# Loading the first batch of a fused attention and feed-forward kernel unit by unit, with GpSimd kept to issuing loads in the opening

## The chip, the cores and the metric

The kernel runs on one core of one Trainium2 chip. The metric is the device time of one execution in microseconds (us); lower is better. The span of a profiled execution is shorter than its time (337.9 against 339.8 us for the kernel before), and both are used here, never one against the other.

## The reference

Causal attention in a sliding window of 64 over 8 batches, 8 heads, 576 positions and 64 channels, then a feed-forward layer with a rectified gate over the 4608 rows:

```
scores = (q @ k^T) / sqrt(64)          # q, k, v: [8, 8, 576, 64] fp32, inputs scaled by 0.1
mask   = (0 <= i - j < 64)
attn   = softmax(where(mask, scores, -1e9)) @ v
x      = attn.transpose(0, 2, 1, 3).reshape(4608, 512)
out    = (relu(x @ w_gate) * (x @ w_val)) @ w_out      # 512 x 1536, 512 x 1536, 1536 x 512
```

## The kernel before

Attention works in 24 **units** of 192 positions (three windows, all 8 heads), three to a batch. Two units make a **tile** of 384 rows of the feed-forward layer. A unit goes through scores (`st`), exp (`p`), the product with v (`pv`, with the sums of the softmax by matmuls with ones), the copy from PSUM (`xv`), and normalisation on VectorE (`sT`, `rT`, `rs`, then `xt`). `xt` is what the gate matmuls (`h<-xt,wg`) read. The **hidden part** of a tile is its gate and value matmuls (`wg`, `wv`), its **output** the matmuls with w_out (`op`). In the first units the mask comes into the scores by **bias** matmuls. **Warm-ups** (`heat`) are matmuls on zeros that keep TensorE busy. To **land** is to have arrived in full. Matmuls of both layers are woven together by a table of times, `W.at(t, ...)`, which sets the program order on each engine.

The opening loads all of batch 0's k and q, four heads to a load, transposes them on VectorE, and does units 0 and 1 side by side:

```python
def k_first(hh):                          # k of batch 0 in fp32 over the sync queue
    k32 = nat["k32", hh] = x_sb.tile([128, S // 32 * D], FP32, name="k32", bufs=2)
    nc.sync.dma_start(k32, k[0, G * hh:G * hh + G].rearrange("h (i j) d -> (h i) (j d)", i=32))
...
def v_load(u):                            # by GpSimd's queue
    b, uu = divmod(u, UB)
    for w in range(UB):
        k0 = U * uu + 64 * w
        nc.gpsimd.dma_start(v16s[uu][64:128, w, :, 0:64], v[b, :, k0:k0 + 64].rearrange("h p d -> p h d"))
... # the schedule of the opening
W.at(8.7, lambda: u_st(0, (0,)))
W.at(11.0, lambda: u_st(0, (1,)))
W.at(11.4, lambda: u_pv(0, (0, 1)))
W.at(11.5, lambda: u_pv(0, (2, 3)))
W.at(11.7, lambda: u_st(1))               # unit 1's scores, ahead of unit 0's normalisation
W.at(12.2, lambda: u_back(0))
W.at(12.5, lambda: u_norm(0))
W.at(12.6, lambda: u_pv(1))
...
W.at(21.0, lambda: v_ones(2, nc.vector))  # memsets of the next v buffers, on VectorE
W.at(21.0, lambda: v_ones(0, nc.vector))
```

The softmax here doesn't subtract the row's maximum and nothing guards it: scores larger than these inputs give would overflow.

## Time and profile before

| what | value |
|---|---|
| time, median (range) | 339.79 us (339.25 to 339.82) |
| profiled span, mean granted clock | 337.9 us, 1.00 but for 3.4 us at 0.50 in the opening |
| k of batch 0 lands | 4.37 and 5.76 us |
| q of batch 0 lands | 7.47 and 9.39 us |
| v of units 0 and 1 lands | 10.02 to 13.00 us |
| first gate matmul | 17.00 us |
| unit 1's first gate matmul | 21.12 us |
| third tile's output starts | 93.92 us, then a steady 25.95 us for most tiles |

"Lands" is the issue's start plus its time to landing in the trace. The prediction shows the page's shares, the chain and the windows. Timeline columns: start us, duration us, engine, source line, operation, written tile <- read tiles, shapes, count, and in brackets the idle time before and its releaser.

```profile
13.13 0.55 PE L249 MATMUL st<-qT,kT 32*128 32x64 f16 x48
...
17.00 2.72 PE L419 MATMUL h<-xt,wg 128*128 128x192 f16 x16 [0.53 <-DVE xt L356]
...
21.12 1.07 PE L419 MATMUL h<-xt,wg 128*128 128x192 f16 x11
```

The first line is unit 1's scores. They are done at 13.7 us, 3.3 us ahead of unit 0's first gate matmul, so that unit 1 follows with no wait on the third line (its x11 are those inside the view's window, of 16). The middle line shows the half clock: 2.72 us for 16 matmuls. Because of it TensorE comes to unit 1 late: unit 1's `xt` is done at 20.46, and its first gate matmul starts at 21.12.

### The profile page before, as it was taken

The page shows a single profiled execution, that of the slowest core. Times are in us where ns is not written, and L with a number is a line of the kernel's source. Part 1 is how long each engine was busy: PE and PEld are TensorE (multiplying, and loading weights), DVE is VectorE, ACT ScalarE, POOL GpSimd, SP SyncE. Part 2 cuts the span into 40 slices and gives each one's busy share as a digit, 9 for nine tenths or more (in the row PEclk, how much of TensorE's full clock was granted, in tenths as well). Part 3 has the DMA queues.
Part 4 walks back from the last instruction along what each step waited for, and adds up shares of the span by engine and source line. Part 5 has one row for each costly group of instructions (what it writes and reads, how often), then busy time and mean ns, then how long its engine had stood idle before and what let it go on. Part 6 is the DMA issues. An engine that isn't in the chain of part 4 may idle for free.

```text
span 337.9 us, 8605 instructions
## 1 busy us (share of the span) xinstructions
PE 325.5 (96%) x3522; PEld 197.3 (58%) x3522; DVE 260.3 (77%) x493; ACT 176.7 (52%) x383; POOL 74.0 (22%) x121
## 2 busy tenths in 40 slices
PE   8699998999999999999999999999999999999995
PEld 4485485856546656655655655654655664664653
DVE  5878878998998874897989974888889874884430
ACT  4546165745636646645555564564564664653321
POOL 8724341250213221320210410150120200000000
PEclk9989999999999999999999999999999999999999
DMA  8999998496343933491242853296214402001002
GB/s 214 178 206 193 204 203 135 31 139 98 24 77 49 158 51 71 29 185 70 17 53 73 111 75 98 18 143 123 17 10 111 32 3 93 2 2 71 24 0 94
DMA packets 52886, 29.44 MB, mean 87 GB/s; under 512 B 39280, under 2 KB 44272, under 8 KB 52848
## 3 DMA queue, kind: packets, MB, share of 16 engines
q0 software_dynamic: 47088, 18.29, 47.4%
q1 hardware_dynamic: 5616, 10.55, 8.7%
q8 instruction: 27, 0.44, 0.6%
q14 instruction: 11, 0.09, 0.1%
q10 hardware_dynamic: 144, 0.07, 0.1%
HBM read 37.75 MB, written 9.44 MB: 140 GB/s over the span
## 4 chain that ended last, share of the span: by engine, by line
PE 81%; DVE 13%; issue 3%; DMA 2%; ACT 0%; DVEq 0%; ACTq 0%; POOLq 0%
PE h L419 52%; PE op L433 21%; PE pv L311 5%; PE st L249 3%; DVE sT L341 2%; DVE qT L186 2%; DMA q<-in_q_dram 2%; DVE g_sb L407 2%; DVE kT L186 1%; DVE xt L356 1%; DVE rs L350 1%; DVE p L270 1%; PE op L465 1%; DVE v L118 1%; DVE rT L348 0%
## 5 line engine op out<-in xcount | busy, mean ns | idle before, releaser
L419 PE MATMUL h<-xt,wg 128*128 128x384 f16 (+1 forms) x640 | 117.5, 313 | 1.7 <-DVE xt L356 1.7
L419 PE MATMUL h<-xt,wv 128*128 128x384 f16 (+1 forms) x640 | 116.7, 311 | 1.0 <-DVE g_sb L407 1.0
L407 DVE TENSOR_TENSOR g_sb<-r_sb,h 128x384 f16<-128x384 f32 x144 | 78.3, 550 | 48.8 <-PE h L419 47.1
L404 ACT ACTIVATE r_sb<-h 128x384 f32<-128x384 f32 x144 | 70.2, 492 | 67.0 <-PE h L419 55.3
L433 PE MATMUL op<-wo,g_sb 128*128 128x512 f16 x420 | 93.0, 379 | 0.0
L192 POOL DMA_DIRECT2D v<-in_v_dram x72 | 49.5, 696 | 181.0 <-PE pv L311 95.3
L419 PEld LDWEIGHTS <-wg 128*128 128x128 f16 x640 | 61.5, 99 | 36.5 <-DVE xt L356 1.6
L419 PEld LDWEIGHTS <-wv 128*128 128x128 f16 x640 | 59.0, 98 | 31.7 <-issue 1.3
L433 PEld LDWEIGHTS <-g_sb 128*128 128x128 f16 x420 | 40.3, 98 | 46.6
L341 DVE STREAM_TRANSPOSE sT<-pv 64x384 f32<-64x384 f32 x88 | 51.1, 580 | 9.7 <-PE pv L311 7.7
L329 ACT COPY xv<-pv 64x384 f32<-64x384 f32 x88 | 41.6, 473 | 21.5 <-DVE sT L341 8.1
L440 ACT COPY o_sb<-op 128x512 f32<-128x512 f32 x35 | 20.5, 586 | 54.6 <-PE op L433 54.6
L263 ACT ACTIVATE p<-st 128x384 f16<-128x384 f32 x92 | 39.7, 492 | 4.2 <-PE st L249 4.1
L270 DVE TENSOR_TENSOR p<-p,mask 128x384 f16<-128x384 f16 x88 | 27.5, 352 | 0.3 <-ACT p L263 0.2
L350 DVE STREAM_TRANSPOSE rs<-rT 128x768 f32<-128x768 f32 x24 | 23.5, 978 | 0.8
L356 DVE TENSOR_TENSOR xt<-xv,rs 128x768 f16<-128x768 f32 x24 | 22.8, 948 | 0.8
L311 PEld LDWEIGHTS <-v 128*128 128x128 f16 x528 | 18.6, 98 | 4.2 <-issue 0.8
L186 DVE STREAM_TRANSPOSE kT<-k 128x576 f32<-128x576 f32 (+1 forms) x18 | 19.7, 1121 | 1.4 <-ACT k L179 1.3
L311 PE MATMUL pv<-p,v 128*128 128x64 f16 x528 | 19.7, 193 | 1.1 <-DVE p L270 0.6
L186 DVE STREAM_TRANSPOSE qT<-q 128x576 f32<-128x576 f32 x16 | 18.9, 1239 | 1.1 <-DMA q<-in_q_dram 1.1
L249 PEld LDWEIGHTS <-kT 32*128 32x128 f16 x1152 | 11.0, 92 | 10.0 <-issue 9.9
L249 PE MATMUL st<-qT,kT 32*128 32x64 f16 x1152 | 13.9, 189 | 2.3 <-DVE qT L186 2.0
(47 smaller groups left out, 91.8 us busy)
## 6 DMA issues: line engine op xcount, KB each, us to landing
out_dram<-o_sb SPq DMA_DIRECT2D x35, 256.0 KB, 2.0
q<-in_q_dram POOLq DMA_DIRECT2D x16, 288.0 KB, 8.1
v<-in_v_dram POOLq DMA_DIRECT2D x72, 64.0 KB, 3.2
k<-in_k_dram POOLq DMA_DIRECT2D x14, 288.0 KB, 6.1
wg<-in_moe_w_gate_dram POOLq DMA_DIRECT2D x3, 512.0 KB, 10.1
wv<-in_moe_w_val_dram POOLq DMA_DIRECT2D x3, 512.0 KB, 11.9
wo<-in_moe_w_out_dram POOLq DMA_DIRECT2D x3, 512.0 KB, 13.7
k<-in_k_dram SPq DMA_DIRECT2D x2, 576.0 KB, 4.0
```

The source lines that it names most:

```text
L186: nc.vector.transpose(dst.rearrange("p (i j) -> p j i", i=32)[:, j0:j1], src[:, j0:j1])
L192: nc.gpsimd.dma_start(v16s[uu][64:128, w, :, 0:64], v[b, :, k0:k0 + 64].rearrange("h p d -> p h d"))
L249: nc.tensor.matmul(d["st"][hh][g][:, c:c + 64], kT[rows, hh, ks + 64 * w:ks + 64 * w + 128, dh], qT[rows, hh, ks + 64 * w:ks + 64 * w + 64 ...
L263: nc.scalar.activation(d["p"][g].rearrange("p h c -> p (h c)"), d["st"][0][g][:, 0:2 * U], ACT.Exp, scale=scale)
L270: nc.vector.tensor_tensor(p, p, mask[:, None, :].to_broadcast([128, 2 * UB, 64]), MUL)
L311: nc.tensor.matmul(d["pv"][c % 2][:, c // 2, e, 64 * w:64 * w + 64], v16[:, w, 128 * h - 64 * e:128 * h - 64 * e + 128], d["p"][h % G][:, ...
L329: nc.scalar.copy(d["xs"][rows, n::2], d["pv"][n][rows, :, e, 0:U])
L341: nc.vector.transpose(to[64 * e:64 * e + 64, half::2], d["pv"][half][64 - 64 * e:128 - 64 * e, :, e, 0:U])
L404: nc.scalar.activation(part(r_sb), part(h1), ACT.Relu)
L407: nc.vector.tensor_tensor(g_sb[:, f:f + w, c0:c1], part(r_sb), part(h2), MUL)
L419: nc.tensor.matmul(h[:, b * n:b * n + n], wt[:, c, (f + b) * 128:(f + b) * 128 + 128], xt[:, c, c0:c1], start=(c == 0), stop=(c == NC - 1))
L433: nc.tensor.matmul(op, g_sb[:, f, bass.ds(sub * 128, 128)], wo[:, f], start=(f == 0), stop=(f == NF - 1))
```

## The change

The intent: unit 0 needs only its own 192 rows of k and q, so load those alone and first (sync queue), flip them on TensorE in place of VectorE, let GpSimd issue nothing but loads until the first tile's weights are under way, and move memsets and copies of v from VectorE to GpSimd. The core of the diff, with cuts marked:

```diff
-    def k_first(hh):
-        k32 = nat["k32", hh] = x_sb.tile([128, S // 32 * D], FP32, name="k32", bufs=2)
-        nc.sync.dma_start(k32, k[0, G * hh:G * hh + G].rearrange("h (i j) d -> (h i) (j d)", i=32))
+    JA = U * H // 128                       # 12: a partition takes 12 positions of one head
+    def all_rows(name, u):
+        src = (q if name == "q" else k)[0, :, U * u:U * u + U]
+        return src.rearrange("h (i j) d -> i h (j d)", j=JA)
+    def unit_flip(name, u):                 # 24 matmuls of 64 columns against a permuted identity
...
+                nc.tensor.matmul(to[64 * hh:64 * hh + 64, 64 * j:64 * j + 64],
+                                 nat[name, u][:, D * j:D * j + D],
+                                 turn[:, G * hh:G * hh + G], ...)
...  (the opening, in program order)
+        for name in "kq":
+            all_load32(name, 0, nc.sync)
+            all_tile(name, 0)
...
+        heat(6, units[0]["st"][3])          # warm-up matmuls
+        for name in "kq":
+            all_load(name, 1)
+        v_load(0, ((1, 0, 128), (3, 0, 64)))
+        v_load(1, ((3, 64, 128), (5, 0, 128)))
+        for wt, t in ((G3[0], 12.3), (V3[0], 14.9), (G3[1], 17.5)):
+            w_load(*wt, t)
...
+        v_fixed(1, nc.gpsimd)               # the memsets, now on GpSimd
+        unit_loads(3)
...
+        v_spread(0)
+        u_st(0)
+        for c in order:
+            u_exp(0, c)
+        heat(6, flipped["k", 0][:, 1])
+        u_pv(0)
...
+        u_back(0)
+        u_norm(0)
+        v_spread(1)
+        heat(3, flipped["k", 0][:, 1])
+        for name in "kq":
+            unit_flip(name, 1)
+            for cc in range(2):
+                unit_keep(name, 1, cc, act)
+        heat(4, flipped["k", 1][:, 1, 256:512])
+        u_bias(1)
+        u_st(1)
+        v_spread(2, pool)
...
-        W.at(21.0, lambda: v_ones(2, nc.vector))
-        W.at(21.0, lambda: v_ones(0, nc.vector))
...
-            output_by_rows(0); ready(3); hidden(1, 0, U)      # abridged
+            ready(3); hidden(1, 0, U); output_by_rows(0)      # abridged
```

## The prediction

> **What bounds the kernel now.** I read the page's busy shares first, then its chain, then three views of the opening: the table of windows, the waits, and the timeline. The page says that TensorE is the bound of the whole:
>
> ```profile
> PE 325.5 (96%) x3522; PEld 197.3 (58%) x3522; DVE 260.3 (77%) x493; ACT 176.7 (52%) x383; POOL 74.0 (22%) x121
> PE 81%; DVE 13%; issue 3%; DMA 2%; ACT 0%; DVEq 0%; ACTq 0%; POOLq 0%
> ```
>
> The second line is the chain that ended last: 81% TensorE, and the 13% VectorE are where a gain could hide. The chain in order of time shows that the steady part is closed: from the third tile on, the 36 output matmuls of successive tiles start at 94.09, 120.04, 146, 172.65, 198.60 us, a period of 25.95 or 26.65 us. Work of one tile: 96 gate and value matmuls of 384 columns at 0.1625 us are 15.6, 36 output matmuls at 0.216 are 7.77, two units of attention at 0.48 + 0.70 are 2.4; 25.8 us. So nine tenths of the span cannot move, and the change must earn its keep before the third tile, at about 75 us. There, three things are lost. The windows of the opening (length, then busy time and count of PE, PEld, DVE, ACT, POOL, then the granted clock, DMA share, GB/s):
>
> ```profile
> 16.64:20.05 3.41, 3.04 (x20) 2.80 (x20) 3.24 (x8) 1.75 (x6) 0.76 (x1) 0.51 1.24 206
> 36.30:54.00 17.70, 17.70 (x208) 12.73 (x206) 14.38 (x25) 7.78 (x17) 7.57 (x12) 1.00 1.50 205
> 54.00:58.20 4.20, 2.80 (x58) 1.32 (x57) 4.12 (x6) 2.46 (x6) 0.08 (x1) 1.00 0.61 53
> 58.20:75.00 16.80, 15.73 (x218) 12.39 (x219) 15.99 (x33) 8.95 (x20) 6.96 (x11) 1.00 0.66 88
> ```
>
> (a) The first feed-forward matmul runs only at 17.0 us, and then at half clock. (b) From 54 to 75 us TensorE idles 2.5 us while VectorE is busy for 20.1 of 21.0: VectorE binds there. (c) Between 24 and 31 us VectorE stands in the chain too, with memsets. The timeline of VectorE in both places:
>
> ```profile
> 14.57 0.30 DVE L348 RECIPROCAL rT<-sT 128x24 f32<-128x24 f32 x1
> 14.91 0.98 DVE L350 STREAM_TRANSPOSE rs<-rT 128x768 f32<-128x768 f32 x1
> 15.99 0.96 DVE L356 TENSOR_TENSOR xt<-xv,rs 128x768 f16<-128x768 f32 x1
> ...
> 24.64 0.48 DVE L116 MEMSET v<- 128x512 f16 x1
> 25.18 1.02 DVE L118 MEMSET v<- 128x512 f16 x2
> 26.36 0.48 DVE L116 MEMSET v<- 64x512 f16 x1
> 26.99 1.03 DVE L118 MEMSET v<- 128x512 f16 x2 [0.15 <-issue]
> ```
>
> The reader sees unit 0's normalisation release the first feed-forward matmul at 17.0, and 3.0 us of memsets in the middle of the gates of tile 0.
>
> Loads are the other limit of the opening. The windows show a steady 206 GB/s written, and one by one the loads land at: k over the sync queue 4.4 and 5.7; q 7.5 and 9.3; v of units 0 and 1 10.0 to 13.0; the six weight blocks of 512 KB 15.0, 18.0, 20.5, 23.1, 25.7, 28.5 (2.6 us apart); v of unit 2 30.1; the three of w_out 32.0, 34.5, 37.1 (issue time plus time to landing, asked for each issue). Their matmuls start at 17.0, 19.5, 23.7, 26.4, 29.6, 33.7 and 36.3, so apart from the first, every weight is there before it is needed.
>
> [...] 0.51 granted in 16.64 to 20.05, a stretch of 3.41 us, after the sparse 13.23 to 16.64; 16 matmuls that take 1.33 us warm took some 2.6 there. [...] No run here shows GpSimd copies yet; the kernel before has none.
>
> **The change, part by part.**
>
> 1. *Smaller first loads.* Unit 0 needs 393 KB each of k and q (fp32) over the sync queue in place of 2 x 590 KB of k there and 2 x 288 KB of q behind GpSimd. At the 332 to 409 GB/s that the windows show from 2 to 5 us, k is in at about 3.7 and q at 4.6 (before: the last q at 9.3).
>
> 2. *Transposes on TensorE.* VectorE's 4.9 us of transposes become 24 matmuls of 64 columns for each of k and q. The old pv and ones matmuls are like them in size: 40 in 1.08 us, 27 ns each; so 0.65 us warm for 24, and copies from PSUM of about 0.5 us each. Estimate: scores at 8.1, the four exps (0.41 each) at 9.5, pv at 10.4 (v lands at about 8.5, its spread ends at 9.2), the four sums to 11.1, then 0.30 + 0.98 + 0.96 as above plus small gaps: xt of unit 0 at about 13.4, against 16.95 now. The first gate block has then landed (estimate 12.8: 2.4 MB read ahead of it, where 3.1 MB were).
>
> 3. *But TensorE and ScalarE first do unit 1's flips and scores.* The four copies of unit 1's k and q (2 us) queue on ScalarE behind unit 0's; I get the scores done at 14.6. **First feed-forward matmul 14.6, against 17.0: 2.4 us won.**
>
> 4. *Unit 1 is then the wait.* Its exps end at 16.0, pv at 16.9, sums 17.5, and 2.3 us of normalisation: xt at 19.7, against 20.46. TensorE has only 0.8 + 2.7 us of work from 14.6 on, and idles from 18.2 to 19.7. Of the 2.4 us about 0.8 is left. [...]
>
> 5. *Unit 2's attention* now stands ahead of the value block: flips 1.3, copies 2 us on ScalarE, bias 0.65, scores 0.5, and 0.7 of waiting. I get the end of tile 0's hidden part at 36.6; before it is 36.3. **At this point nothing is won.**
>
> 6. *VectorE is relieved.* Gone from it between 17 and 75 us: 3.0 us of memsets, v copies of units 2 to 5 (3 x 0.7 plus 0.9), unit 2's masks (1.4). GpSimd takes the memsets and copies, and issues nothing late: units 3, 4, 5 land at about 32, 44 and 51 and are needed at 39, 48 and 56. From 36.3 on, TensorE's work to the third tile's start is 7.8 + 8.0 + 8.0 + 7.8 + 3 x 1.3 = 35.5 us, and it takes 38.6 now. So 3.1 us of gaps is the stake. VectorE's list for that stretch in the new program order comes to some 35 us (12 half gates 6.6, 4 gates 2.2, 12 transposes of 192 columns 6, masks 4, sums 7, three normalisations 6.7, two transposes of the next batch 2.5), as much as TensorE has. So it will not all come back: I take 2 of 3.1.
>
> Sum: 0.3 lost at 36 us, about 2 won by 75, and some 0.6 for the third tile, which has 1.2 us of gaps beyond its 18 us of work: -2.3 us, from 339.8 to **337.5**.
>
> **The rivals.**
>
> *Everything overlaps as planned.* If ScalarE's copies hide and unit 1 comes at 18, the gain is 4 to 5 us (335): it would be bounded by the 5.4 us lost now between 17 and 75. For it: the warming matmuls placed between the steps. Against it: 5 us of ScalarE copies and exps in one line.
>
> *The half clock moves behind unit 1.* [...]
>
> *GpSimd becomes the bound.* Copies slower than I assume[...] delay v or the loads of units 4 and 5, and unit 5 has 5 us of margin only: 340 to 342. Against it: GpSimd is 22% busy, and the DMA share falls to 0.6 after 54 us.
>
> *VectorE stays the bound to 75 us*, so nothing of the 3.1 comes back: 339.5.
>
> **Range and chances.** The gain cannot well exceed 5.5 us, since the steady period stands on TensorE's work; 2% is 6.8 us. So faster by over 2% gets 0.05. A loss of 2% would need a late load for every unit of the first two tiles: 0.02. The range is the middle of the rivals, 334.8 to 340.4.
>
> **What would show it.** Right: first feed-forward matmul at 14 to 15; a TensorE gap of 1 to 2 us ahead of unit 1's gates; hidden part of tile 0 done at 36 to 37; the third tile's gates starting at 72 to 74 rather than 74.8; the period of 25.95 unchanged after it. Wrong: unit 1's first gate matmul well before 19 (gain larger), a clock of 0.5 anywhere after 20 us, VectorE or TensorE waiting on k, q or v of units 3 to 5, or periods after 100 us that differ from before, which I have assumed they do not.

## The result and the profile after

The changed kernel takes **341.48 us** (median; 340.92 to 341.85, four runs) against 339.79: a ratio of 1.0052, with a 95% interval of 1.0033 to 1.0071. A ratio is the mean time of one kernel's fast runs over that of the other's of the same rounds, so it is not quite the ratio of the medians. By the 2% rule it is "the same", but the sign is the opposite of the predicted one. The profiled span is 339.5 us against 337.9.

The page's shares and chain, after:

```profile
PE 326.7 (96%) x3593; PEld 197.6 (58%) x3593; DVE 251.6 (74%) x486; ACT 177.4 (52%) x387; POOL 77.7 (23%) x114
PE 67%; DMA 15%; DVE 7%; POOL 6%; issue 4%; ACT 0%; POOLq 0%; DVEq 0%; ACTq 0%
```

VectorE has lost 8.7 us of work, yet the span grew. DMA in the chain went from 2% to 15%: the chain of waits now runs back through loads and GpSimd. A chain is one way back of several, so I looked for when each thing happened. TensorE's timeline of the opening, after:

```profile
11.82 0.25 PE L357 MATMUL pv<-p,v 128*64 128x64 f16 x4 [0.51 <-DVE v L265]
...
17.03 0.52 PE L305 MATMUL st<-qA,kA 64*128 64x64 f16 x24
17.49 1.50 PE L487 MATMUL h<-xt,wg 128*128 128x192 f16 x16
...
23.14 1.07 PE L487 MATMUL h<-xt,wg 128*128 128x192 f16 x11 [1.91 <-DVE xt L423]
```

Unit 1's scores stand at 17.03 us, where they stood at 13.13, and its first gate matmul at 23.14, where it was 21.12; ahead of it TensorE idles for 1.91 us on VectorE's `xt`. The half clock is gone: 1.50 us for 16 matmuls, and the granted clock is 1.00 in every window of the table below. What led there, on ScalarE and VectorE:

```profile
4.96 0.51 ACT L214 CAST ka<-k 128x384 f16<-128x384 f32 x1 [2.66 <-DMA k<-in_k_dram]
...
6.17 0.51 ACT L214 CAST qa<-q 128x384 f16<-128x384 f32 x1 [0.70 <-DMA q<-in_q_dram]
...
11.34 0.42 DVE L265 COPY v<-v 64x1024 f16<-64x1024 f16 x1 [2.35 <-DMA v<-in_v_dram]
...
15.56 0.96 DVE L423 TENSOR_TENSOR xt<-xv,rs 128x768 f16<-128x768 f32 x1
...
22.13 0.96 DVE L423 TENSOR_TENSOR xt<-xv,rs 128x768 f16<-128x768 f32 x1
```

k, q and unit 0's v are waited for until 4.96, 6.17 and 11.34 us; the two last lines are the `xt` of units 0 and 1. The windows that answer to those in the prediction (length, busy time and count of PE, PEld, DVE, ACT, POOL, then clock, DMA share, GB/s):

```profile
17.49:23.14 5.65, 3.75 (x70) 3.35 (x65) 3.47 (x8) 3.41 (x10) 5.09 (x6) 1.00 1.52 186
23.14:28.00 4.86, 4.86 (x54) 3.89 (x55) 1.99 (x4) 1.96 (x4) 4.06 (x5) 1.00 1.24 205
...
48.20:61.38 13.18, 12.56 (x148) 6.63 (x146) 10.35 (x22) 7.09 (x16) 8.62 (x11) 1.00 0.69 107
61.38:71.50 10.12, 9.58 (x169) 9.28 (x168) 9.76 (x20) 7.07 (x16) 6.97 (x12) 1.00 1.07 161
```

TensorE idles 1.90 us in the first of them, and 1.16 us in the two last together (48.2 to 71.5 us), where it had idled 2.5 us between 54 and 75 us before. By stages, each an interval between two starts in the traces:

| stage | before | after | difference |
|---|---|---|---|
| start to unit 1's first gate matmul | 21.12 | 23.14 | +2.02 |
| from there to the end of tile 0's hidden part | 15.17 | 16.59 | +1.42 |
| from there to the third tile's first gate matmul | 38.48 | 36.96 | -1.52 |
| from there to the third tile's output | 19.15 | 19.21 | +0.06 |
| from there to the end | 243.98 | 243.57 | -0.41 |
| sum (span) | 337.90 | 339.47 | +1.57 |

(The end of tile 0's hidden part is the start of the work behind it: of its output at 36.29 us before, and of tile 1's gates at 39.73 after, as the output of tile 0 stands at another place in the program order there.) The 1.4 us more in tile 0's hidden part are work of TensorE: it is busy for 16.33 of 16.59 us, and for 14.68 of 15.17 before; unit 2's flips and bias are in there now. From unit 1's first gate matmul to the third tile's output it is 72.80 us before and 72.76 after. This interval is 72.7 to 73.0 in every variant of the changed kernel below but dve_back, though the milestone itself moves from 19.6 to 26.9, so **unit 1's first gate matmul** is the milestone by which they can be read. It also says that the loads and GpSimd work in the chain are not what ended last up to the third tile: in vf_early everything comes 3.5 us earlier, and the interval stays.

### The profile page after: what moved, and what is told of

The parts are those of the page before. It is cut to its first block, busy times and chain, and to the rows that moved or that the text cites.

```text
span 339.5 us, 8693 instructions
## 1 busy us (share of the span) xinstructions
PE 326.7 (96%) x3593; PEld 197.6 (58%) x3593; DVE 251.6 (74%) x486; ACT 177.4 (52%) x387; POOL 77.7 (23%) x114
## 4 chain that ended last, share of the span: by engine, by line
PE 67%; DMA 15%; DVE 7%; POOL 6%; issue 4%; ACT 0%; POOLq 0%; DVEq 0%; ACTq 0%
PE h L487 43%; PE op L501 18%; DMA v<-in_v_dram 13%; PE pv L378 4%; DMA q<-in_q_dram 3%; PE st L318 2%; DVE qT L250 2%; DVE sT L408 2%; POOL v L267 1%; POOL qu L190 1%; POOL v L265 1%; POOL ku L190 1%; DVE xt L423 1%; PE op L533 1%; DVE kT L250 1%
## 5 line engine op out<-in xcount | busy, mean ns | idle before, releaser
L256 POOL DMA_DIRECT2D v<-in_v_dram x41 | 34.4, 845 | 116.5 <-PE pv L378 81.1
L408 DVE STREAM_TRANSPOSE sT<-pv 64x384 f32<-64x384 f32 x84 | 48.8, 581 | 9.7 <-PE pv L378 7.8
L396 ACT COPY xv<-pv 64x384 f32<-64x384 f32 x84 | 39.6, 471 | 19.8 <-DVE sT L408 7.9
L328 ACT ACTIVATE p<-st 128x384 f16<-128x384 f32 x96 | 41.5, 491 | 8.1 <-PE st L318 6.8
L378 PE MATMUL pv<-p,v 128*128 128x64 f16 x504 | 18.5, 193 | 0.3 <-DVE p L338 0.3
L318 PEld LDWEIGHTS <-kT 32*128 32x128 f16 x1008 | 9.8, 92 | 9.2 <-issue 8.5
L250 DVE STREAM_TRANSPOSE kT<-k 128x576 f32<-128x576 f32 x12 | 14.7, 1238 | 0.2
L318 PE MATMUL st<-qT,kT 32*128 32x64 f16 x1008 | 12.5, 189 | 2.4 <-DVE qT L243 1.2
L250 DVE STREAM_TRANSPOSE qT<-q 128x576 f32<-128x576 f32 x12 | 14.1, 1237 | 0.0
```

The source lines that it names most:

```text
L250: nc.vector.transpose(dst.rearrange("p (i j) -> p j i", i=32)[:, j0:j1], src[:, j0:j1])
L256: nc.gpsimd.dma_start(v16s[b % 2][lo:hi, g, :, 0:64], v[b, :, 64 * g - 64 + lo:64 * g - 64 + hi].rearrange("h p d -> p h d"))
L318: nc.tensor.matmul(d["st"][g][:, c:c + 64], kT[rows, hh, ks + 64 * w:ks + 64 * w + 128, dh], qT[rows, hh, ks + 64 * w:ks + 64 * w + 64, dh ...
L328: nc.scalar.activation(d["p"][g].rearrange("p h c -> p (h c)"), d["st"][g][:, 0:2 * U], ACT.Exp, scale=scale)
L378: nc.tensor.matmul(d["pv"][c % 2][:, c // 2, e, 64 * w:64 * w + 64], v16[:, w, 128 * h - 64 * e:128 * h - 64 * e + 128], p_of(u, h)[:, 64 ...
L396: nc.scalar.copy(d["xs"][rows, n::2], d["pv"][n][rows, :, e, 0:U])
```

## The experiments

My first theory: the loads of unit 0 and the order unit 0 before unit 1 make unit 1 late. The rivals: GpSimd's copies and memsets disturb VectorE or hold up loads, or VectorE's relief is worth less than thought. Calls ran on several chips, each beside the kernel before, whose medians there were 338.78 to 339.71 us; so ratios are compared, not times across calls; a difference of spans or milestones is one between single profiled executions, so where the timed runs differ from it, the text gives both. Milestones of all runs, from the traces (us):

| run | first gate matmul | unit 1's first gate matmul | third tile's output | span | ratio to the kernel before, 95% |
|---|---|---|---|---|---|
| before | 17.00 | 21.12 | 93.92 | 337.90 | |
| changed | 17.49 | 23.14 | 95.90 | 339.47 | 1.0052 [1.0033, 1.0071] |
| changed, again | 17.53 | 23.19 | 95.99 | 339.55 | 1.0060 [1.0029, 1.0090] |
| early1 | 22.10 | 26.68 | 99.44 | 342.98 | 1.0122 [1.0077, 1.0166] |
| early1_late | 18.58 | 22.71 | 95.44 | 339.01 | 1.0103 [1.0079, 1.0128] |
| early2 | 17.82 | 21.23 | 94.06 | 337.60 | 1.0020 [1.0005, 1.0035] |
| v_first | 16.55 | 22.21 | 94.96 | 338.50 | 1.0006 [0.9991, 1.0021] |
| vf_early | 16.22 | 19.62 | 92.38 | 335.92 | 0.9980 [0.9961, 0.9999] |
| vf_early_again | 16.36 | 20.46 | 93.23 | 336.79 | 0.9983 [0.9969, 0.9996] |
| vf_early_act | 16.17 | 20.47 | 93.34 | 337.12 | 1.0016 [0.9998, 1.0034] |
| dve_back | 17.15 | 22.81 | 98.23 | 341.80 | 1.0135 [1.0117, 1.0152] |
| memset_alone | 16.81 | 20.31 | 102.26 | 345.81 | 1.0250 [1.0235, 1.0266] |
| memset_early | 16.63 | 20.13 | 93.48 | 337.02 | 0.9992 [0.9974, 1.0011] |
| half_rows (wrong result) | 16.02 | 21.68 | 94.43 | 337.98 | one look |
| contig (wrong result) | 16.16 | 21.81 | 94.57 | 338.13 | one look |
| grouped (wrong result) | 16.61 | 22.27 | 95.08 | 338.62 | one look |
| strided (wrong result) | 17.03 | 22.69 | 95.44 | 338.99 | one look |
| head_major | 20.63 | 26.91 | 99.73 | 343.30 | 1.0144 [1.0113, 1.0175] |
| vf_early_hm | 18.35 | 21.86 | 94.64 | 338.21 | 1.0074 [1.0033, 1.0114] |
| early2_hm | 21.53 | 25.82 | 98.78 | 342.36 | 1.0135 [1.0102, 1.0169] |

One thing blurs the milestones. The half clock of the opening differs between executions of one kernel: while unit 0's gates ran, the granted clock was 0.50 for some 3.4 us in the profiles of before, early1_late, early2_hm, vf_early_act and vf_early_again, for longer in early1, and 1.00 in the others. In vf_early and vf_early_again unit 1's `xt` is done at 19.56 alike, but its gates start at 19.62 and 20.46.

The four kernels marked wrong read the wrong rows, to time the loads. They passed the comparison all the same, so it says nothing of which rows unit 0 and 1 read; I suppose (it was only argued) that it is because inputs scaled by 0.1 make all weights of the softmax nearly equal.

### Unit 1 earlier: early1, early1_late, early2

early1 puts unit 1's flips, bias and scores ahead of unit 0's pv, with half of the copies on VectorE:

```diff
-        heat(6, flipped["k", 0][:, 1])
+        for name in "kq":
+            unit_flip(name, 1)
+        for name in "kq":
+            unit_keep(name, 1, 0, dve)
+            unit_keep(name, 1, 1, act)
+        heat(8, flipped["k", 1][:, 1, 256:512])
+        v_spread(0)
+        u_bias(1)
+        u_st(1)
         u_pv(0)
+        for c in order:
+            u_exp(1, c)
...  (removed further down; unit 1's pv 1.6 us earlier in the table)
```

> Unit 1's flips, copies, bias and scores are moved ahead of unit 0's pv, into the stretch where TensorE waits for v; half of the copies go to VectorE. Theory O (order: unit 1's attention stands serially behind unit 0's, so its xt comes at 23.1 us instead of 20.5): unit 1's scores end near 12.5 us instead of 17.5, the first gate matmul starts at about 16.6, xt of unit 1 is ready at 20 to 20.5, and the time falls by about 2.5 to 3 us against the changed kernel (341.5 to about 338.7). Theory L (loads: v that lands at 11.3 us sets all that follows): xt of unit 1 moves by under 1 us and the time stays within 1 us of 341.5.

It missed: 344.68 us. The timeline of early1 at the place where it stopped:

```profile
17.69 2.38 DVE L265 COPY v<-v 64x512 f16<-64x512 f16 x1
17.88 2.04 POOL L124 MEMSET v<- 128x2304 f32 x1
20.73 0.32 PE L357 MATMUL pv<-p,v 128*64 128x64 f16 x4 [6.00 <-DVE v L267]
```

A copy of v on VectorE, 0.29 us in the changed kernel, took 2.38 while GpSimd's memset ran for 2.04. TensorE waited for 6.00 us, and the granted clock was 0.50 from 19.4 to 26 us. That the memset held the copy up was so far only inferred, from their overlap (17.88 to 19.92 us). Two runs test the cause. early1_late moves the memset alone (both diffs here are against early1):

```diff
-        v_fixed(1, nc.gpsimd)
         unit_loads(3)
+        v_fixed(1, nc.gpsimd)
```

> As early1, but GpSimd's memset of 2 us stands behind unit 3's loads instead of ahead of them, so it runs a few us later. Theory (the VectorE copy that took 2.38 us was held by the memset, since they overlap from 17.88 to 19.92): the copy at about 17.7 takes 0.29 us again and the time falls from 344.7 by about 2 us. Rival (the copy waited for its data, v of unit 1): it stays at 2 us or more and the time does not move.

The copy and the memset in early1_late:

```profile
17.00 0.29 DVE L265 COPY v<-v 64x512 f16<-64x512 f16 x1
...
24.23 2.04 POOL L124 MEMSET v<- 128x2304 f32 x1
```

With the memset away from it the copy is back at 0.29 us, and TensorE's wait is 3.62 us in place of 6.00: the collision was the cause of 2.4 us of early1's pause. The other 3.62 us are order again: unit 1's copy of v stands behind unit 0's normalisation on VectorE, which ends at 16.96. Its median is still 342.21; the profiled execution, 340.85 us, was the fastest of four, so its span of 339.01 flatters it, though it has the half clock too (from 18.2 to 21.7 us). early2 instead moves unit 1's copy of v ahead of the memset:

```diff
         v_spread(0)
+        v_spread(1)
         u_bias(1)
...
-        v_spread(1)
         v_spread(2, pool)
```

> As early1, but the v copies for unit 1 come right behind those for unit 0, so they do not meet GpSimd's memset at 17.9 us, where one of them took 2.38 us in place of 0.29. Theory O (order): with that out of the way unit 1's scores at 13.2 us are worth what early1 was to show: pv of unit 1 by about 15.5, its xt at 20 to 20.5, and about 338.7 us. If the time stays at 341 or above, the serial order of the two units was not the loss.

339.70 us, 1 us above what was expected: unit 1 comes at 21.23, 1.9 us earlier than in the changed kernel, and the span is 1.9 us shorter. By the ratios (1.0020 against 1.0052) it is 1.1 us. So the **order of unit 0 and unit 1** is worth 1 to 2 us, once nothing holds the copy up.

### The loads: v_first, half_rows

v_first only issues unit 0's v ahead of unit 1's k and q:

```diff
         bands()
+        v_load(0, ((1, 0, 128), (3, 0, 64)))
         for name in "kq":
             all_load(name, 1)
-        v_load(0, ((1, 0, 128), (3, 0, 64)))
```

> GpSimd issues unit 0's two v loads ahead of unit 1's k and q. Theory L: v lands about 2 us earlier (9 us or so instead of 11.2), pv of unit 0 starts at about 10 instead of 11.8, and the first gate matmul, unit 1's xt and the whole time come 1.5 to 2 us earlier (about 339.7). Theory O: xt of unit 0 comes earlier, but unit 1's k and q land about 1 us later (12.3 and 10.6 at least), so unit 1's xt gains under 1.5 us, and the time with it.

v lands at 8.41 us in place of 11.24, but unit 0's pv starts only at 11.58 (11.82 before this edit): unit 0's exps come first, and then six warm-up matmuls of 512 columns, which start at 9.46 and take 2.19 us. `xt` of unit 0 is done at 15.58 (16.52), unit 1's first gate matmul is at 22.21. So 2.8 us of landing gave 1.0 us of span. Part of this is the clock of this one execution: the first warm-ups start 0.40 to 0.43 us apart and the last 0.22, and the granted clock is 0.50 from 8 to 11 us. The exps had ended at 10.72. By the ratios (1.0006 against 1.0052) v_first is worth 1.6 us.

half_rows reads half of unit 0's k and q, with a wrong result:

```diff
-        queue.dma_start(t32, all_rows(name, u))
+        queue.dma_start(t32[:, 0:JA * D // 2], all_rows(name, u)[:, :, 0:JA * D // 2])
```

> Wrong result on purpose: only the first half of each row of unit 0's k and q is loaded (1536 bytes in place of 3072) and used twice. If bytes set the time of these loads, k lands about 0.6 us and q about 1.2 us earlier than 4.93 and 6.14, as half of 786 KB at the 340 GB/s seen is 1.2 us less. If rows (packets) or the start set it, both stay within 0.4 us, and so do unit 1's k and q behind them (8.15 and 9.22).

k lands at 3.95 (4.93), q at 4.52 (6.14), v at 9.72 (11.24), and the span is 337.98, 1.5 us shorter. The first loads are on the path. (k and q gained more than the 0.6 and 1.2 us that the bytes alone were to give. TensorE was also at full rate early here, see step 2 below.)

### Both together: vf_early, its repetition, and another queue for q

vf_early combines v_first and the early unit 1, with unit 0's pv ahead of unit 1's bias and scores, and unit 1's copy of v in the gap of VectorE ahead of unit 0's reciprocal:

```diff
+        v_load(0, ((1, 0, 128), (3, 0, 64)))
         for name in "kq":
             all_load(name, 1)
-        v_load(0, ((1, 0, 128), (3, 0, 64)))
...
-        heat(6, flipped["k", 0][:, 1])
+        for name in "kq":
+            unit_flip(name, 1)
+        for name in "kq":
+            unit_keep(name, 1, 0, dve)
+            unit_keep(name, 1, 1, act)
         u_pv(0)
+        heat(6, flipped["k", 1][:, 1, 256:512])
+        u_bias(1)
+        u_st(1)
         u_sum(0, 0)
...
+        v_spread(1)
+        for c in order:
+            u_exp(1, c)
         u_back(0)
         u_norm(0)
```

> v of unit 0 ahead of unit 1's k and q, and unit 1's flips ahead of unit 0's pv, with unit 1's v copies ahead of unit 0's reciprocal: both causes taken away at once. Theories L and O together: xt of unit 0 at about 15, first gate matmul at 15.1 (the first weight block lands at 14.9), xt of unit 1 at about 18.6 instead of 23.1, so 337 to 338 us, below both kernels. If only one of them counts, 338.5 to 340.

Unit 1's normalisation and first gate matmul in vf_early:

```profile
18.60 0.96 DVE L423 TENSOR_TENSOR xt<-xv,rs 128x768 f16<-128x768 f32 x1
...
19.62 1.49 PE L487 MATMUL h<-xt,wg 128*128 128x192 f16 x16 [0.58 <-DVE xt L423]
```

The same two lines stood at 22.13 and 23.14 us in the changed kernel. The wait is down to 0.58 from 1.91 us, and from here to the third tile's output it takes 72.76 us, as in the changed kernel: all 3.5 us reach the end of the span. `xt` of both units came about 1 us later than expected (15.90 and 19.56). It beats both kernels: 338.26 us, 0.9980 of the time before; against the changed kernel that is 2.4 us by the ratios. The gain over the kernel before is small, so it ran again in more rounds:

> A repeat of the kernel with v first and unit 1's flips early, for an interval: 0.2 to 0.5% below the kernel before, its profiled span near 335.9 against 337.9.

338.67 us, 0.9983 [0.9969, 0.9996]: the gain holds, at a fifth of a per cent. (The profiled execution had unit 1's first gate matmul 0.84 us later than the first profile. The half clock does it: unit 0's 16 gate matmuls took 2.74 us in place of 1.49, while unit 1's `xt` was done at 19.56 in both.) And once with unit 0's q issued by ScalarE's queue:

```diff
-            all_load32(name, 0, nc.sync)
+            all_load32(name, 0, nc.sync if name == "k" else nc.scalar)
```

> As vf_early, with unit 0's q issued from ScalarE's queue, ahead of the table load, so that it does not wait 0.73 us for SyncE to issue k. If the start of the loads is on the path, q lands 0.3 to 0.7 us earlier than 6.57, unit 1's first gate matmul comes as much earlier than 19.62, and the time falls by 0.3 to 0.7 us. If the DMA engines are full from the start, all landings stay and so does the time.

q was issued 0.7 us earlier (0.81 us) but landed only 0.3 earlier (6.27 against 6.57), unit 1's k and q landed 0.4 and 0.7 later, and the time was not better (1.0016).

### VectorE's relief: dve_back, memset_alone, memset_early

dve_back returns memsets and copies of v to VectorE within the changed kernel:

```diff
-        v_fixed(1, nc.gpsimd)
+        W.at(21.0, lambda: v_fixed(1, nc.vector))
...
-        v_spread(2, pool)                  # likewise units 3, 4, 5
+        W.at(25.0, lambda: v_spread(2))
...
-        v_fixed(0, nc.gpsimd)
+        W.at(38.0, lambda: v_fixed(0, nc.vector))
```

> GpSimd's memsets and v copies are put back on VectorE, at the times that the kernel before had them; everything else as changed. Theory: the part from the end of tile 0's hidden block to the third tile took 37.0 us against 38.5 before because of this relief; so with it undone that part takes 38 to 38.5 again and the time grows by about 1 to 1.5 us (about 342.8). Rival: the shorter part comes from the order of work (unit 3's gates ahead of tile 0's output), and the time stays within 0.5 us of 341.5.

344.38 us, a ratio of 1.0135 where the changed kernel has 1.0052, and 2.3 us more of span, though unit 1 is 0.33 us earlier; from unit 1's first gate matmul to the third tile's output it is 75.4 us in place of 72.8. So in the new order this move of work to GpSimd is worth 2.6 us or so by the traces (2.8 by the ratios), more than I expected, though GpSimd takes 0.61 us for a copy of 64x512 that VectorE does in 0.29. Its memsets by themselves, in the kernel before (`k_zeros` moves too):

```diff
-        W.at(21.0, lambda: v_ones(2, nc.vector))
-        W.at(21.0, lambda: v_ones(0, nc.vector))
+        W.at(21.0, lambda: v_ones(2, nc.gpsimd))
+        W.at(21.0, lambda: v_ones(0, nc.gpsimd))
```

> The kernel before with one part of the change alone: its memsets between 24 and 28 us go from VectorE to GpSimd, in the same places of the program. Theory (VectorE's 3 us there are on the path to the end of tile 0): the hidden block of tile 0 ends 0.4 to 0.8 us earlier and the time falls by as much, 339.1 or so. Rival: GpSimd runs them between w_out's loads and the next batch's, holds those loads back by 2 us or slows VectorE's copies, and the time stays or grows by up to 1 us.

Much slower, 347.65 us. In memset_alone:

```profile
36.16 0.54 POOL L116 MEMSET v<- 128x512 f16 x1
36.75 0.23 PE L311 MATMUL pv<-p,v 128*128 128x64 f16 x1 [6.54 <-POOL v L116]
```

GpSimd's memsets stood in its program behind loads that wait for buffers, until 36.16 us, and TensorE waited 6.54 us for one. memset_early puts them right behind the loads of w_out, ahead of those of the next batch:

```diff
-        W.at(21.0, lambda: v_ones(2, nc.vector))
-        W.at(21.0, lambda: v_ones(0, nc.vector))
-        W.at(22.0, k_zeros)
+        W.at(12.85, lambda: v_ones(2, nc.gpsimd))
+        W.at(12.86, lambda: v_ones(0, nc.gpsimd))
+        W.at(12.87, k_zeros)
```

> The kernel before with its memsets on GpSimd, as memset_alone, but placed right behind w_out's loads and ahead of the next batch's, so that they do not stand behind waits for landings (there they ran only at 36.2 us and pv of unit 2 waited 6.5 us). Theory (VectorE's 3 us between 24 and 28 us lie on the path to the end of tile 0): the hidden block of tile 0 ends 0.5 to 0.8 us earlier and the time falls by as much against before. Rival (the later gates and the unit's sums absorb it): within 0.3 us of before.

338.87 us, 0.9992 [0.9974, 1.0011]: no gain that can be told from none. The hidden part of tile 0 took 15.42 us with the 3 us of memsets off VectorE, and 15.17 with them on it. (Its profiled span is 0.9 us shorter than before's; half of that is there at the third tile's output, and this execution did not have the half clock.) So in the kernel before, as far as one profile goes, the memsets were **not** what held tile 0's hidden part, although VectorE stood in the chain there.

### How the rows lie: contig, head_major, strided, grouped

The prediction timed the first loads at rates seen in the kernel before. There a load reads one block of memory, since four whole heads lie one behind the other. The changed kernel reads 128 rows of 3072 B with the head as the fast index, so that neighbouring rows lie far apart. contig reads as many rows from one block, for units 0 to 2 (wrong result):

```diff
-        src = (q if name == "q" else k)[0, :, U * u:U * u + U]
-        return src.rearrange("h (i j) d -> i h (j d)", j=JA)
+        n = 128 * JA * D
+        src = (q if name == "q" else k)[0].rearrange("h s d -> (h s d)")[n * u:n * u + n]
+        return src.rearrange("(i j) -> i j", j=JA * D)
```

> Wrong result on purpose: the same rows of 3072 bytes of k and q for units 0 to 2, but read as one contiguous block, where the change reads them head by head in turn. If the head-interleaved layout is what slows these loads (issue 0.67 us where the kernel before had 0.40, first landing 4.13 us after issue for 393 KB where 590 KB took 3.56), the issue takes 0.40 again, k and q land by about 4.2 and 5.3, and v 1 us earlier. If the size of the rows or the sharing between the queues does it, the landings stay within 0.3 us of 4.93, 6.14 and 11.24.

k lands at 3.83 and q at 4.76 us: the predicted 3.7 and 4.6, within 0.2. v lands at 9.60, and the span is 1.3 us shorter. Then a layout with a right result, in which a head's rows stay together:

```diff
-        nc.vector.tensor_copy(turn, ident.rearrange("p (i h) -> p h i", h=H))
+        nc.vector.tensor_copy(turn, ident.rearrange("p (h i) -> p h i", h=H))
...
-        return src.rearrange("h (i j) d -> i h (j d)", j=JA)
+        return src.rearrange("h (i j) d -> h i (j d)", j=JA)
```

> The changed kernel with one thing altered and a right result: unit rows lie head after head over the partitions (16 pieces of one head, then the next head) in place of head by head in turn, and the constant matrix of the flips is permuted to match. If it is the turning through the heads that slowed the loads (contig, all in one block, had k at 3.83 and v at 9.60), k lands by 4.0, q by 4.9, v by 9.8, the first gate matmul of unit 1 comes at 21.8 instead of 23.1, and the time falls by 1.2 to 1.5 us. If only a fully contiguous block is fast, the landings stay near 4.93, 6.14 and 11.24 and the time stays.

It missed: 344.71 us; k was waited for until 6.33 and q until 9.63. The busy share of the DMA engines from 0 to 12 us in 40 slices, and the sync queue's packets, in the changed kernel:

```profile
DMA  0000000994599989899799999999999999999999
...
q1 hardware_dynamic: 288, 0.79, 24.0%
```

and in head_major:

```profile
DMA  0000000732447555557989999999999999999999
...
q1 hardware_dynamic: 272, 0.79, 23.3%
```

The engines are about half busy while k and q are read. The 288 packets are 256 rows and 32 packets of 4 B, 16 for each of the two loads; in head_major there are 16 of them, 8 for each load. The slowest dimension of the source here is 8 heads, and was 16 groups of positions. No run altered that dimension alone (contig, strided and grouped, with 128, 128 and 16, have 288 packets like the changed kernel), so it is not shown what lowered the busy share. But as it fell together with the change of layout, the run says nothing of the rows themselves. Two more with the same layout suffered alike (vf_early_hm is 2.3 us of span slower than vf_early, early2_hm 4.8 than early2), beside a repetition of the changed kernel that agreed with the first:

> The head-major layout with v first and unit 1's flips early: if loads and order add up, unit 1's first gate matmul at about 19 instead of 20.5 or 19.6, and 337 to 337.8 us where vf_early had 338.3 to 338.7. If the weights (first block at 13.4 to 13.5, second at 16.7) or VectorE's chain bind by then, it equals vf_early.

> The head-major layout with unit 1's flips early and v behind unit 1's k and q, as the change has it: if the layout alone brings v early enough, this equals vf_early_hm within 0.5 us; if v first still counts, it is 0.5 to 1.5 us slower.

> The changed kernel itself, as the base for the others of this set: within 0.3 us of 341.5, or as much lower as the kernel before is in this set.

Two last runs, both with wrong results and 16 or 128 as the slowest dimension, take the two remaining causes apart. strided has rows that don't touch but one even step; grouped has 16 groups of 8 touching rows, so a pattern of two levels as in the changed kernel:

```diff
# strided
+        n = JA * D
+        flat = (q if name == "q" else k)[0].rearrange("h s d -> (h s d)")
+        return flat.rearrange("(i r) -> i r", i=128)[:, n * u:n * u + n]
# grouped
+        n = 8 * JA * D
+        flat = (q if name == "q" else k)[0].rearrange("h s d -> (h s d)")
+        return flat.rearrange("(o r) -> o r", o=16)[:, n * u:n * u + n].rearrange("o (i j) -> o i j", i=8)
```

> A wrong result on purpose: unit 0's and 1's q and k rows are read as 128 rows of 3072 B that lie at one even step of 9216 B, so that the source is one row pattern as in the contiguous run, but no two rows touch. In the contiguous run k took 0.39 us to issue and landed at 3.83 us, q at 4.76; in the changed kernel 0.67, 4.93 and 6.14. If what delays the changed kernel is that its pattern has two levels (heads inside positions), this run stays near the contiguous one: issue about 0.4, k at 3.8 to 4.1, q at 4.7 to 5.1, span 338.1 to 338.4. If it is that neighbouring rows don't touch in memory, k lands at 4.6 to 5.0 and q at 5.8 to 6.2 whatever the issue took, span 339 to 339.5.

> A wrong result on purpose: the same rows read as 16 groups of 8 rows, the 8 rows of a group next to one another in memory, the groups 73.7 KB apart, so that the source has two levels like the changed kernel's, with 16 on the outside, but neighbouring rows touch. If the two-level pattern is what costs, the issue takes about 0.67 us again and k lands at 4.6 to 5.0 us, q at 5.8 to 6.2, span 339 to 339.5. If the cost is in rows that don't touch, k lands at 3.8 to 4.2 and q at 4.7 to 5.1, span about 338.2. If both this run and the strided one stay near the contiguous run, it is the turn from head to head alone that costs; if both are late, each costs by itself.

The issues of k on the sync queue, in strided, grouped and the changed kernel (duration of the issue as min/median/max in ns, then the time to landing):

```profile
L209 SPq DMA_DIRECT2D k<-in_k_dram x1: 384/384/384, 0.8 to 0.8; - x1
...
DMA to landing us min/median/max: 3.4/3.4/3.4
```

```profile
L209 SPq DMA_DIRECT2D k<-in_k_dram x1: 684/684/684, 0.8 to 0.8; - x1
...
DMA to landing us min/median/max: 4.4/4.4/4.4
```

```profile
L208 SPq DMA_DIRECT2D k<-in_k_dram x1: 673/673/673, 0.8 to 0.8; - x1
...
DMA to landing us min/median/max: 4.1/4.1/4.1
```

| run | pattern, rows | k lands | q lands | unit 0's v lands | unit 1's first gate matmul | span |
|---|---|---|---|---|---|---|
| contig | one level, touching | 3.83 | 4.76 | 9.60 | 21.81 | 338.13 |
| grouped | two levels, touching by eights | 5.18 | 6.73 | 10.30 | 22.27 | 338.62 |
| strided | one level, apart | 4.18 | 5.09 | 10.80 | 22.69 | 338.99 |
| changed | two levels, apart | 4.93 | 6.14 | 11.24 | 23.14 | 339.47 |

Neither expectation came true alone. The **two-level pattern** lengthens the issue from 0.38 to 0.67 us (the first packet starts at 2.3 us in place of 1.8) and delays k and q on the sync queue: by 0.75 and 1.05 us with rows apart (strided to changed), by 1.35 and 1.97 with touching rows (contig to grouped). **Rows apart** delay unit 0's v, which comes behind unit 1's k and q: by 1.20 us with one level (contig to strided), by 0.94 with two (grouped to changed). On unit 1's first gate matmul the pattern is worth 0.46 us, the rows 0.88, and both together 1.33, so they add up. These are single looks, and the rate of TensorE before 10 us was not the same in them (the four bias matmuls of unit 0 took 0.82 us in grouped and 1.46 in the other three); the changed kernel's two looks differ by 0.05 us at this milestone. The step between rows is 9216 B in strided and a whole head, 147 KB, in the changed kernel; whether the size of the step matters was not tried.

## Why the prediction was wrong

The kernel was predicted at 337.5 us, in a range that ended at 340.4, and took 341.48. What failed is the path of unit 0, steps 1 and 2: its `xt` was said for 13.4 us and came at 16.52, 1.3 us of it by the loads and 1.8 by the work behind them. Step 4 hands that on, and the gain counted behind it (steps 5 and 6) was too small to make up for it. By its own steps:

**Step 1, smaller first loads: failed.** "k is in at about 3.7 and q at 4.6", v "at about 8.5"; measured 4.93, 6.14 and 11.24. The rate was taken from loads that read one block, and applied to rows far apart in a two-level pattern. With a block of memory (contig) k and q were as estimated, and `xt` of unit 0 came at 15.18 in place of 16.52: 1.3 us of the miss. Even then v came at 9.60, 1.1 us later than said; with v issued ahead of unit 1's k and q (v_first) it came at 8.41.

**Step 2, transposes on TensorE: half right.** The flips cost what was estimated (0.85 us for 24 matmuls of unit 0, 0.55 to 0.57 for those of unit 1, against 0.65), but the path from loads to `xt` was too short: 13.4 us was said, and contig, with k and q on time, gets 15.18. That is 1.8 us more. In contig's trace the exps end at 10.5 (9.5 estimated), so 1.0 of the 1.8 us is there by then. Its beginning can be read:

```profile
4.78 0.51 ACT L215 CAST qa<-q 128x384 f16<-128x384 f32 x1 [0.41 <-DMA q<-in_q_dram]
5.43 1.46 PE L276 MATMUL st<-bias,ident 128*128 128x384 f16 x4
6.82 0.85 PE L225 MATMUL qf<-turn,qa 128*64 128x64 f16 x24
```

q's cast is done at 5.29, but its flips start at 6.82, behind unit 0's four bias matmuls, which the estimate leaves out. And TensorE runs at half rate there: in half_rows the same four and the 24 flips read

```profile
5.36 0.82 PE L275 MATMUL st<-bias,ident 128*128 128x384 f16 x4
6.12 0.57 PE L224 MATMUL qf<-turn,qa 128*64 128x64 f16 x24
```

(The granted clock is given as 1.00 in both.) Further on, v's copies end at 11.0 (9.2 estimated), and six warm-up matmuls stand ahead of pv until 11.2, which I had taken for filling only. In v_first, where v came at 8.41, they and the exps alone kept pv until 11.58. No run took the bias matmuls or the warm-ups out of the way, so how these share the 1.8 us is open.

**Step 3, first feed-forward matmul at 14.6: right in mechanism, wrong by 2.9 us**: it comes right behind unit 1's scores (17.03), as said, but inherits steps 1 and 2 (17.49). From `xt` of unit 0 to it, 1.2 us were estimated and 0.97 measured.

**Step 4, unit 1 is then the wait: right in mechanism.** The gap ahead of unit 1's gates is there, 1.91 us in the trace (1.5 estimated), and from unit 0's `xt` to unit 1's it takes 6.57 us (6.3). But the start was 3.1 us late: `xt` of unit 1 at 23.09 in place of 19.7. In sum 3.4 us: 1.3 from the layout of the loads, 1.8 from the short path, 0.3 here. The wait could be removed by order: vf_early, by v first and unit 1 early, brings this `xt` to 19.56 (and the wait to 0.58 us).

**Step 5, tile 0's hidden part at 36.6: wrong, 39.73**, 3.1 us later, by what step 4 handed on; from unit 1's `xt` to there it took 16.6 us, against 16.9 estimated.

**Step 6, VectorE's relief: right in direction.** 1.5 us of the 2 came back between tile 0's hidden part and the third tile (the stage takes 36.96 us, 36.6 predicted). dve_back shows that the work moved to GpSimd is worth 2.6 us in this order, so something else in the new order takes part of it back; which part, no run tells. The further 0.6 us "for the third tile" did not come at all (19.15 before, 19.21 after), and I had no mechanism for it. Both stakes were differences of sums, and too large: TensorE idled 2.5 us in the first of these stages before (3.1 assumed), and 0.5 us in the second (1.2 assumed).

So the miss of 4.0 us is 3.39 from step 4, 0.36 from step 6 and 0.66 from the third tile, less 0.26 in step 5 and 0.41 behind the third tile's first output; the last 0.26 is the median's distance from the profiled execution. **The rivals:** the half clock did not move behind unit 1 (clock 1.00 after 14 us in both profiles of the changed kernel; my estimate for it was 339 us, from half of the 3.41 us that the kernel before spent at 0.51), GpSimd held TensorE up in early1 and memset_alone, but in the changed kernel no wait of TensorE is put down to it, and "everything overlaps" failed for the same reasons as step 1. The periods after the third tile did not change for the worse (25.94 us), as assumed. One of the three losses read from the profile was no loss: no gain was seen when the memsets were taken off VectorE in the kernel before (memset_early). A smaller reading does not hold either: the first weight block was there in time as well (landed at 15.0, used at 17.0).

## What to carry to other kernels

A rate seen in a trace belongs to the pattern of the load that made it (k landed at 3.83 us from one block and at 4.93 from rows apart in two levels): before it is applied to other rows, compare how many levels the pattern has, whether rows touch, and how busy it keeps the DMA engines (about half in head_major, where k was waited for until 6.33 us in place of 4.96). When two units lead into the main loop, time the second one: in the new order every microsecond of its first gate matmul came out at the end. Moving its scores ahead of the first unit's normalisation was worth 1 to 2 us, as much as a change of the loads (v_first 1.0 to 1.6, half_rows 1.5); which is worth more, these runs cannot tell. Where a clock differs between executions (0.50 or 1.00 here while unit 0's gates ran), read it before two profiles are compared. Before work is moved to another queue, look at what stands ahead of it there (in memset_alone a memset stood behind loads until 36.16 us) and at what runs beside it (in early1 a copy on VectorE took 2.38 us in place of 0.29 beside a memset on GpSimd).
